# A routing table in SBUF, built from products of one-hot matrices, in a kernel of attention and two MoE layers

## The chip, the cores and the metric

The kernel runs on one core of a Trainium2 chip. The metric is the device time of one execution in microseconds. Engines: TensorE (PE in the profile; its weight loads are PEld), VectorE (DVE), ScalarE (ACT), GpSimd (POOL), and SyncE (SP), which issues most DMAs.

## The reference

Attention with a feature map, on 8 batches of 8 heads with 576 rows of 64, then two MoE layers on the 4608 rows of 512 that come out, each with 8 experts and one expert per row:

```python
def phi(x):
    proj = np.einsum('bhsd,df->bhsf', x, w_phi)
    proj = proj - np.max(np.abs(proj), axis=-1, keepdims=True)
    return np.concatenate([np.exp(proj), np.exp(-proj)], axis=-1)
q_p, k_p = (phi(q), phi(k))
kv = np.einsum('bhsf,bhsd->bhfd', k_p, v)
z = np.sum(k_p, axis=2)
num = np.einsum('bhsf,bhfd->bhsd', q_p, kv)
den = np.einsum('bhsf,bhf->bhs', q_p, z)[..., None] + 1e-06
...
logits = x @ w_gate + modality_bias[modality_id]
e_idx = np.argmax(logits, axis=1)
...
    h = np.maximum(x[mask] @ w1[e], 0.0)
    out[mask] = gate_w[mask, None] * (h @ w2[e])
```

The second layer is like the first, with another gate on its output. The inputs are float32.

## The kernel before

The work is written out in order by hand, so the order of the code is the order of each engine's queue. A small class `weave` holds chains of VectorE operations and puts a few of them between other work (`weave.step`), or all that is left of one (`weave.finish`).

**Attention** runs as 72 units, t = 9 b + s: in unit t the features of k for the s-th part of batch b are made (proj, km, kd, kp), while older units' sums over k (`kv_head`, line 1297, 128 columns per matmul) and output sums (`num`, line 1382, 65 columns) are under way. A unit of 8 heads x 4 chunks of v has its ones column apart, in `ONES`, so that the sum of k_p comes with the product. `num` ends in den, a reciprocal, and xt on VectorE (lines 1362 to 1366).

**Routing of a batch** is behind it: logits (`x_logits`, line 376), `finish` (softmax, one-hot matrix of the expert), `x_store` (rows to DRAM, line 1537), `x_ranks` (matmuls, lines 337 and 339), `places` (VectorE, lines 345 to 360: for each row its place in a table of 36864 numbers, ordered by expert), `x_enter`. `enter` (line 365) is, per chunk of 128 rows, an indirect DMA of GpSimd that scatters 128 numbers of 4 bytes into one of several tables in DRAM; the number names the row. The tables are zeroed first (line 444). Batches 0 to 5 do this inside the units of the following batches (the finish at t = 9 b + 24 or 25, the scatter at 9 b + 26), batches 6 and 7 in a tail behind the units, between the first MoE tiles.

**MoE** runs over 40 tiles of 128 rows per layer. A tile gathers its rows by an indirect DMA (line 752) whose indices come from the table. Three tiles of the fullest expert come early: `early_rows` reads their part of the tables (line 562), `early_idx` makes indices. At the end `route_a` reads five whole tables back (line 620), and `route_b` picks from them by 30 matmuls with one-hot columns (line 699). Lines 782 to 784 and 802 to 806 are the tiles' matmuls. The second layer has its own tables and the same steps.

Of the kernel before, what the change touches and what calls it, by code (L numbers as in the profile page):

```python
# [23 lines left out]
F = 128  # L24
# [20 lines left out]
PI = 1.0 / PS  # L45
V = D + 1

ONES = 32 * D + 8 * V

CM = 5  # L50

# [2 lines left out]
def attention_two_moe(  # L54
# [13 lines left out]
    x2_d = dpool.tile([NSLOT * 128 + 1, XW], F32, name="x2_d")  # L68
    rows_of = [C1 * 128, NSLOT * 128]

    tab_d = [[dpool.tile([NROW, 1], F32, name=f"tab{n}_{k}") for k in range(K)] for n, K in enumerate((5, G))]

    whole = ((0, 1),)

# [36 lines left out]
    row_no = []  # L111
    for n in range(2):
# [6 lines left out]
        row_no.append(t.rearrange("p c t -> p (c t)").bitcast(F32))  # L119

    nxt = [iota(f"nxt{n}", [[NT, NE]]) for n in range(2)]
    row0 = iota("row0", [[NT, NE]])
# [219 lines left out]
    def places(ps, oh16, C, n, valid=None):  # L342

        pl = sp.tile([128, CM, NE], F32, tag="pl", name="pl")[:, 0:C]
        nc.vector.tensor_tensor(
            pl, ps[:, 0:C], nxt[n].unsqueeze(1).to_broadcast([128, C, NE]), op=ALU.add)
        nc.vector.tensor_tensor(nxt[n], nxt[n], ps[:, C], op=ALU.add)
        yield
        nc.vector.tensor_tensor(pl, pl, oh16[:, 0:C], op=ALU.mult)
        yield  # L350
        po = sp.tile([128, CM], F32, tag="po", name="po")[:, 0:C]
        nc.vector.tensor_reduce(out=po, in_=pl, op=ALU.add, axis=AX.X)
        yield
# [8 lines left out]
        return pi  # L362

    def enter(n, pi, c, r):
        nc.gpsimd.indirect_dma_start(
# [35 lines left out]
    v1s = [flat(f"v1_{i}", 4 * (ONES + D)) for i in range(2)]  # L401
    w_m = [[flat(f"w{w}_{i}", 8192) for i in range(2)] for w in range(2)]


# [113 lines left out]
    etab = [const.tile([128, len(tab_d[n]), E], F32, name=f"etab{n}") for n in range(2)]  # L518
    ereg = {}

    def early(n):
# [45 lines left out]
    def early_idx(n):  # L567
        s = sp.tile([128, E, 2], F32, tag="es", name="es")
        nc.vector.tensor_reduce(
            out=s, in_=etab[n].rearrange("p k c -> p k c").bitcast(F16).rearrange("p k (c t) -> p c t k", t=2),  # L570
            op=ALU.add, axis=AX.X)
        yield
        nc.vector.scalar_tensor_tensor(
            out=s[:, :, 1], in0=s[:, :, 0], scalar=128.0, in1=s[:, :, 1], op0=ALU.mult, op1=ALU.add)
        yield
        nc.vector.tensor_scalar(eidx[n], s[:, :, 1], float(rows_of[n]), None, op0=ALU.add)
        yield
# [113 lines left out]
    def route_b(n):  # L691


        tab16, sel, ntile, ex = routed[n, "a"]
        rows = state["pg"][:, 3, 0 : 2 * M].rearrange("p (t m) -> p t m", t=2)
        for x in range(2):
            for i, t in enumerate(tab16):
                for k in range(3):
                    nc.tensor.matmul(  # L699
                        rows[:, x], t[:, k, :, x], sel[:, k], start=(i == 0 and k == 0),  # L700
                        stop=(i == len(tab16) - 1 and k == 2))
        rs = rt(n, "rs", [128, M])
        nc.vector.tensor_scalar(rs, rows[:, 0], 128.0, float(rows_of[n]), op0=ALU.mult, op1=ALU.add)
        idx = rt(n, "idx", [128, M], I32, True)
        nc.vector.tensor_tensor(idx, rs, rows[:, 1], op=ALU.add)
# [412 lines left out]
    with ExitStack() as actx:  # L1118
# [3 lines left out]
        sm = actx.enter_context(tc.tile_pool(name="sm", bufs=2))  # L1122
        def vw(t, u):

            a = t[:, D * u : D * u + D]
            return bass.AP(a.tensor, a.offset, [a.ap[0], (ONES - D * u, 2), (1, D)])

        def v_rem(t):


            return view(t, F32, 32 * D, 4, 2, V)

        weave = Weave()

# [30 lines left out]
        def load_v(b, half):  # L1165
            v1 = v1s[b % 2]
            if b < 2 and not half:
                nc.gpsimd.memset(v1[:, ONES:], 1.0)
                nc.gpsimd.memset(v_rem(v1), 0.0)
                for t in range(2):  # L1170
                    nc.gpsimd.memset(v_rem(v1)[64 * t : 64 * t + 64, :, t, D:V], 1.0)
            for c in (2 * half, 2 * half + 1):
                nc.sync.dma_start(
                    out=view(v1, F32, 0, H, 4, D)[:, :, c],
                    in_=v[b, :, 128 * c : 128 * c + 128].rearrange("h p d -> p h d"))
# [113 lines left out]
        def kv_head(b, h):  # L1289

            v1, kp = v1s[b % 2], kps.pop((b, h))
            if h % 2 == 0:
                kvp[b] = bank("kv", F32, 2, 2, 2 * D)
            ps = kvp[b]
            for half in range(2):
                for c in range(4):
                    nc.tensor.matmul(  # L1297
                        ps[:, half, h % 2], kp[:, c, half, :], vw(v1, 4 * h + c),
                        start=(h % 2 == 0 and half == 0 and c == 0), stop=False)
            if h % 2:  # L1300
# [223 lines left out]

        def x_places(b):
            n = 4 + b % 2
            rows[b, "pi"] = yield from places(rows[b, "rk"], rows[b, "oh"], n, 0)

        def x_enter(b):
            pi = rows.pop((b, "pi"))  # L1530
            for c in range(4 + b % 2):
                enter(0, pi, c, 9 * (b // 2) + 4 * (b % 2) + c)

        def x_store(b):
            for c, r in rows[b]:
# [24 lines left out]
        for t in range(9 * B + 6):  # L1560
# [41 lines left out]
            if b + 2 < B and s in (5, 6):  # L1602
                load_qk(q_of(b + 2), qT[b + 2], s - 5)
            split_step(split0, weave, t, "load")
            ready = batch_at(23)
            if ready != B - 3:
                ready = batch_at(24)
                ready = None if ready == B - 3 else ready
            if ready is not None:
                weave.finish(chains.pop(("finish", ready)))  # L1610
                x_store(ready)
# [54 lines left out]
            for x in firsts[t][1:] if 4 <= t < 9 else []:  # L1666
                proj(q_proj(*x))
                q_max(*x)
            each(5, num)
            if at(18, 0) and at(18)[0] < B - 1:  # L1670
                x_logits(*at(18))
            if at(17, 0) and at(17)[0] < B - 1:
                a_T(*at(17))
            if ready is not None:
                x_ranks(ready)
                chains["places", ready] = weave.add(x_places(ready))
# [15 lines left out]
            weave.step()  # L1692
            if ready is not None:
                weave.finish(chains.pop(("places", ready)))
            entered = ready if ready == B - 3 else batch_at(26)
            if entered is not None and (entered, "pi") in rows:
                x_enter(entered)

            if t == 9 * B - 3:
                chains["early"] = weave.add(early(0))  # L1700
            if t == 9 * B - 2:
                weave.finish(chains.pop("early"))
                early_rows(0)
            if t == 9 * B + 1:
                done(early_idx(0))
                for i in range(E):
                    gather(0, i)
            if t in (9 * B + 1, 9 * B + 5):
# [41 lines left out]
        x_enter(last)  # L1750


    late = ctx.enter_context(tc.tile_pool(name="late", bufs=1))
# [85 lines left out]
```

## Time and profile before

| | us |
|---|---|
| runs: median (lowest, highest) | 1561.77 (1560.21, 1566.68) |
| profiled execution | 1563.24 |
| its span, first to last instruction | 1561.5 |
| TensorE busy | 1467.9 (94%) |
| VectorE busy | 746.4 (48%) |
| ScalarE busy | 553.4 (35%) |
| GpSimd busy | 228.3 (15%) |
| mean granted clock of TensorE | 0.958 |

The attention runs to about 536 us, the tail with the first tiles to about 590, the MoE layers from there. A busy share is a mean over all of it: what a stage waits for is read from the waits and windows of that stage. The clock is given as a share of 2.4 GHz; a mean between 0.5 and 1 in a window is a mixture of stretches at 1.2 and at 2.4 GHz.

### The profile page before, as it was taken

What the parts mean: (1) busy time and instruction counts of PE and PEld (TensorE: products, weight loads), DVE (VectorE), ACT (ScalarE), POOL (GpSimd) and SP (SyncE); (2) the same over time, 40 slices, a digit from 0 to 9 for tenths busy, and PEclk for the clock granted to TensorE, in tenths of its full rate; (3) what the DMA queues carried; (4) which work ended last, traced back from release to release, by engine and by line L of the source; (5) the groups of instructions that cost most, each with busy time, mean ns of one, the idle gap of its engine ahead of it and who ended that gap; (6) DMA issues with size and microseconds to landing.
All of it is one profiled execution on the core that took longest, in us unless ns stands there. A gap on an engine that the chain in (4) does not pass through costs nothing. (4 is left out here: it accounts for less than half of the span.)

```text
span 1561.5 us, 38909 instructions
## 1 busy us (share of the span) xinstructions
PE 1467.9 (94%) x15626; PEld 1157.4 (74%) x15626; DVE 746.4 (48%) x2255; ACT 553.4 (35%) x850; POOL 228.3 (15%) x273
## 2 busy tenths in 40 slices
PE   6999998987999879999999999799889999999998
PEld 4999998987989847667777776466657777777775
DVE  3668776757756434646665666354341111111111
ACT  1346565554555403334444444243211111111111
POOL 1000101101011121202211211120131211211221
PEclk8999998989989889999999999899999999999999
DMA  8255656677431753657667777678945353484381
GB/s 250 92 159 164 142 170 157 174 168 136 124 62 49 265 84 114 158 185 201 204 213 178 195 180 230 113 199 244 306 150 174 76 150 104 133 272 138 81 281 43
DMA packets 158268, 254.40 MB, mean 163 GB/s; under 512 B 90953, under 2 KB 95613, under 8 KB 152192
## 3 DMA queue, kind: packets, MB, share of 16 engines
q1 hardware_dynamic: 141264, 210.22, 50.2%
q0 software_dynamic: 14784, 41.44, 7.9%
q8 instruction: 127, 2.08, 0.7%
q14 instruction: 61, 0.50, 0.1%
q10 hardware_dynamic: 2032, 0.16, 0.1%
HBM read 428.60 MB, written 83.22 MB: 328 GB/s over the span
## 5 line engine op out<-in xcount | busy, mean ns | idle before, releaser
L784 PE MATMUL proj<-xT,w 128*128 128x128 f16 x896 | 154.8, 221 | 10.4 <-issue 10.4
L783 PE MATMUL proj<-xT,w 128*128 128x128 f16 x896 | 154.7, 221 | 6.1 <-issue 6.1
L782 PE MATMUL proj<-xT,w 128*128 128x128 f16 x896 | 154.6, 220 | 3.2 <-issue 3.2
L802 PE MATMUL num<-w,qs 128*128 128x512 f32 x336 | 151.6, 605 | 0.0
L794 DVE SCALAR_TENSOR_TENSOR qs<-proj,qs 128x512 f16<-128x512 f32 x54 | 37.4, 692 | 228.3 <-ACT qs L793 228.3
L784 PEld LDWEIGHTS <-w 128*128 128x128 f16 x1344 | 132.2, 98 | 18.6 <-issue 18.6
L802 PE MATMUL num<-ks,qs 128*128 128x512 f32 x304 | 140.1, 614 | 4.2 <-DMA ks<-in_moe_w_dram 4.2
L1382 PE MATMUL num<-kvsb,E 128*128 128x65 f32 x1024 | 129.6, 282 | 11.9 <-DVE xt L1366 11.8
L782 PE MATMUL proj<-xT,v 128*128 128x128 f16 x816 | 138.7, 219 | 0.7 <-DVE xT L771 0.7
L784 PE MATMUL proj<-xT,v 128*128 128x128 f16 x816 | 138.7, 219 | 0.2 <-issue 0.2
L783 PE MATMUL proj<-xT,v 128*128 128x128 f16 x816 | 138.7, 219 | 0.0
L782 PEld LDWEIGHTS <-w 128*128 128x128 f16 x1344 | 132.1, 98 | 8.4 <-issue 4.4
L1382 PEld LDWEIGHTS num<-kvsb,E 128*128 128x128 f32 x1024 | 125.6, 200 | 14.9 <-issue 8.3
L1297 PE MATMUL kv<-v,kp 128*128 128x128 f32 x1024 | 135.7, 288 | 0.5 <-issue 0.5
L783 PEld LDWEIGHTS <-w 128*128 128x128 f16 x1344 | 132.1, 98 | 4.0 <-issue 2.0
L752 POOL DMA_INDIRECT xg<-x_d,idx x74 | 77.6, 1049 | 388.7 <-PE px L371 189.5
L1297 PEld LDWEIGHTS kv<-v,kp 128*128 128x128 f32 x1024 | 126.6, 201 | 1.6 <-issue 1.6
L783 PEld LDWEIGHTS <-v 128*128 128x128 f16 x1216 | 118.9, 98 | 3.1 <-issue 1.0
L782 PEld LDWEIGHTS <-v 128*128 128x128 f16 x1216 | 118.9, 98 | 2.5 <-issue 0.4
L784 PEld LDWEIGHTS <-v 128*128 128x128 f16 x1216 | 118.9, 98 | 0.0
L802 PEld LDWEIGHTS num<-w,qs 128*128 128x128 f32 x336 | 63.3, 193 | 72.0 <-issue 72.0
L1205 PE MATMUL proj<-wps,ks 64*128 64x128 f32 (+1 forms) x640 | 113.9, 301 | 0.9 <-issue 0.6
(328 smaller groups left out, 3366.7 us busy)
## 6 DMA issues: line engine op xcount, KB each, us to landing
w<-pl SPq DMA_DIRECT2D x114, 1024.0 KB
v<-pl SPq DMA_DIRECT2D x80, 1024.0 KB
ks<-in_moe_w_dram SPq DMA_DIRECT2D x40, 1024.0 KB
ks<-pl SPq DMA_DIRECT2D x40, 1024.0 KB
w<-in_moe_w_dram SPq DMA_DIRECT2D x38, 1024.0 KB
wf<-in_moe_w_dram SPq DMA_DIRECT2D x64, 512.0 KB
pl<-wo SPq DMA_DIRECT2D x52, 512.0 KB
w<-in_moe_w_dram SPq DMA_DIRECT2D x32, 512.0 KB
```

The source lines that it names most:

```text
L752: nc.gpsimd.indirect_dma_start(out=xg(n, i), out_offset=None, in_=src[n][0:nr, :], in_offset=bass.IndirectOffsetOnAxis(ap=ix, axis=0), bou ...
L782: nc.tensor.matmul(h[:, j], wk[:, 0, cs], xT[:, k], start=(k == 0), stop=False)
L783: nc.tensor.matmul(h[:, j], wk[:, 0, cs], xT[:, 4 + k], start=False, stop=False)
L784: nc.tensor.matmul(h[:, j], wk[:, 1, cs], xT[:, k], start=False, stop=(k == 3))
L794: nc.vector.scalar_tensor_tensor(out=lo, in0=h, scalar=0.0, in1=hi, op0=ALU.max, op1=ALU.subtract)
L802: nc.tensor.matmul(y, h[:, k], wk, start=(k == 0), stop=(k == 7))
L1205: nc.tensor.matmul(*a, **kw)
L1297: nc.tensor.matmul(ps[:, half, h % 2], kp[:, c, half, :], vw(v1, 4 * h + c), start=(h % 2 == 0 and half == 0 and c == 0), stop=False)
L1382: nc.tensor.matmul(ps[:, c, 0:V], e[:, half, 128 * c : 128 * c + 128], kw(g, half), start=(half == 0), stop=(half == 1))
```

## The change

1. The first layer's table lies in SBUF as `tab0`, [96, 3, 128] in f16. A number's place p is split into p & 127 and the rest (three more VectorE operations in `places`). For each chunk, `hots` makes two one-hot matrices: 128 x 128, scaled by a code of the row, and 128 x 288. `tab_add` multiplies them on TensorE, three matmuls per chunk, and `tab_out` adds the result to `tab0` on VectorE. Nothing of it goes through DRAM; the five tables of this layer, their zeroing, their scatters and their reads are gone. The second layer keeps its tables.
2. Picking: three matmuls (`tab_pick`), then three VectorE operations that turn the f32's bits into a row number (`decode`), for the early tiles and for `route_b`.
3. Places: batches 0 to 5 finish all at t = 9 b + 24 (s = 6); the one-hots are finished and multiplied at 9 b + 25 (s = 7), ahead of `num`. The early tiles' indices come one unit earlier.
4. In units with s = 1, `num` comes behind `x_logits` and `a_T`.
5. v lies with 65 columns per unit, its own ones column among them, so the matmuls of the sums over k have 65 columns in place of 128.
6. The tail: batch 6's logits of the last batch come first, then one-hots and table; behind batch 7's ranks, places, one-hots and table follow with no tile between.

```diff
+    tab0 = const.tile([96, 3, 128], F16, name="tab0")
+    nc.gpsimd.memset(tab0, 0.0)
...
+        nc.vector.tensor_scalar(pi, pi, 127, None, op0=ALU.bitwise_and)
+        pk = sp.tile([128, CM], F32, tag="pk", name="pk")[:, 0:C]
+        nc.vector.tensor_copy(pk, pi)
+        nc.vector.tensor_tensor(po, po, pk, op=ALU.subtract)
+        return pk, po
+    def hots(at_, pk, po, c0, mems):
+        out_ = []
+        at_.append(out_)
+        for c, m in enumerate(mems):
+            a, o = m[:, 0:128], m[:, 128:416]
+            nc.vector.tensor_scalar(
+                a, iota128, pk[:, c : c + 1], code[:, c0 + c : c0 + c + 1], op0=ALU.is_equal, op1=ALU.mult)
+            nc.vector.tensor_scalar(o, iota_c, po[:, c : c + 1], None, op0=ALU.is_equal)
+            out_.append((a, o))
+            yield
+    def tab_add(tag, hs_):
+        ps = bank(tag, F32, 3, 128)
+        for k in range(3):
+            for i, (a, o) in enumerate(hs_):
+                nc.tensor.matmul(
+                    ps[0:96, k], o[:, 96 * k : 96 * k + 96], a, start=(i == 0), stop=(i == len(hs_) - 1))
+        return ps
+    def tab_out(ps):
+        nc.vector.tensor_tensor(tab0, tab0, ps[0:96], op=ALU.add)
+    def decode(out_, ps, tag, w):
+        bits = sp.tile([128, w], I32, tag=tag, name="bits", bufs=1)
+        nc.vector.tensor_scalar(bits, ps.bitcast(I32), 13, None, op0=ALU.logical_shift_right)
+        nc.vector.tensor_scalar(bits, bits, -1.0, float((137 << 10) + 5119), op0=ALU.mult, op1=ALU.add)
+        nc.vector.tensor_scalar(out_, bits, float(rows_of[0]), None, op0=ALU.min)
...
+    def tab_pick(ps, sel):
+        for k in range(3):
+            nc.tensor.matmul(ps, tab0[:, k], sel[:, k], start=(k == 0), stop=(k == 2))
...
+        if n == 0:
+            tab_pick(rows[:, 0], sel)
+            done(decode(idx, rows[:, 0], "bits", M))
...
-            a = t[:, D * u : D * u + D]
-            return bass.AP(a.tensor, a.offset, [a.ap[0], (ONES - D * u, 2), (1, D)])
+            return t[:, V * u : V * u + V]
...
-                        ps[:, half, h % 2], kp[:, c, half, :], vw(v1, 4 * h + c),
+                        ps[:, half, h % 2, 0:V], kp[:, c, half, :], vw(v1, 4 * h + c),
...
-            for c in range(4 + b % 2):
-                enter(0, pi, c, 9 * (b // 2) + 4 * (b % 2) + c)
+        def x_enter(b, tag="qf"):
+            rows[b, "pt"] = tab_add(tag, rows.pop((b, "hots")))
...
-            ready = batch_at(23)
-            if ready != B - 3:
-                ready = batch_at(24)
-                ready = None if ready == B - 3 else ready
+            ready, entered = [(t - x) // 9 if (t - x) % 9 == 0 and 0 <= (t - x) // 9 < B - 2 else None for x in (24, 25)]
...
-            each(5, num)
+            if entered is not None:
+                weave.finish(chains.pop(("hots", entered)))
+                x_enter(entered)
+                tab_out(rows.pop((entered, "pt")))
+            if s != 1:
+                each(5, num)
             if at(18, 0) and at(18)[0] < B - 1:
                 x_logits(*at(18))
             if at(17, 0) and at(17)[0] < B - 1:
                 a_T(*at(17))
+            if s == 1:
+                each(5, num)
...
-            entered = ready if ready == B - 3 else batch_at(26)
-            if entered is not None and (entered, "pi") in rows:
-                x_enter(entered)
+                chains["hots", ready] = weave.add(x_hots(ready))
+                weave.step(2)
...
-        x_enter(last - 1)
-        tiles()
         for c in range(n):
             x_logits(last, c)
+        done(x_hots(last - 1))
+        x_enter(last - 1)
+        tab_out(rows.pop((last - 1, "pt")))
+        tiles()
...
         done(x_places(last))
-        x_enter(last)
+        done(x_hots(last))
+        x_enter(last, "num2")
+        tab_out(rows.pop((last, "pt")))
```

How the order moves. VectorE's queue of before, from batch 4's places (L352, po; L360, pi) into the next unit (den and xt finish an output sum, km and kd belong to k, nm to q):

```order
L352 TENSOR_REDUCE po<-pl 128x4
L244 SCALAR_TENSOR_TENSOR wo<-w_1_155,sb,wo 128x1024
L360 CAST pi<-po 128x4
L1362 TENSOR_SCALAR den<-num 128x4
L1268 TENSOR_REDUCE km<-proj 128x4
L1364 RECIPROCAL den<-den 128x4
L1225 TENSOR_REDUCE nm<-proj 128x4
L1366 TENSOR_TENSOR xt<-num,den 128x4x64
L1274 TENSOR_TENSOR kd<-proj,km 128x512
L1449 TENSOR_REDUCE xm_4850<-xmx 128x4
```

VectorE's queue of the changed kernel, from the same unit's xt and kd on (line numbers are those of the changed file: L1443 is xt, L1351 kd; L392 and L394 make the one-hots, in borrowed memory called kd):

```order
L1443 TENSOR_TENSOR xt<-num,den 128x4x64
L1351 TENSOR_TENSOR kd<-proj,km 128x512
L199 TENSOR_SCALAR pb<-pb 128x5
L1521 TENSOR_REDUCE xmx<-xt 128x4
L202 TENSOR_SCALAR sb<-pb 128x5
L203 TENSOR_SCALAR xi<-pb 128x5
L392 TENSOR_SCALAR kd<-iota_81,pk,code 128x128
L394 TENSOR_SCALAR kd<-iota_c,po 128x288
```

Three more pairs of L392 and L394 follow, and `tab_out`; before, these places held no such operation, and batch 4's entry was on GpSimd.

TensorE's queue of before, behind the ranks of batch 7 in the tail (L339 are the last ranks, L782 the first matmuls of a tile):

```order
L339 MATMUL pl<-oh_6363,ones_81 128x16
L339 LDWEIGHTS ones_81
L339 MATMUL pl<-oh_6363,ones_81 128x8
L782 LDWEIGHTS w_0_154
L782 MATMUL kv<-xT_145,w_0_154 128x128
```

TensorE's queue of the changed kernel at that place (L351 are the ranks, L402 the matmuls of `tab_add`, weights first):

```order
L351 MATMUL pl<-oh_6480,ones_76 128x16
L351 LDWEIGHTS ones_76
L351 MATMUL pl<-oh_6480,ones_76 128x8
L402 LDWEIGHTS kprem
L402 MATMUL num_6524<-kprem 96x128
```

Where a tile's matmuls stood behind the ranks, the table's matmuls stand now, 15 of them, and the tile comes behind those.

## Rows read from the trace of the kernel before

**Rows 1.** The page, part 1: engines, busy us, share of the span, instructions.

```profile
PE 1467.9 (94%) x15626; PEld 1157.4 (74%) x15626; DVE 746.4 (48%) x2255; ACT 553.4 (35%) x850; POOL 228.3 (15%) x273
```

**Rows 2.** TensorE's waits from 150 to 540 us: total us, times, longest.

```profile
PE num L1382 <- DVE xt L1366: 9.2, 10, 2.5
PE proj L1205 <- issue: 8.3, 4, 7.4
PE pl L376 <- issue: 4.3, 2, 3.7
PE qf L1340 <- issue: 3.6, 3, 1.5
PE qf L1205 <- issue: 3.0, 1, 3.0
PE px L371 <- issue: 1.7, 1, 1.7
```

**Rows 3.** TensorE's waits from 540 to 600 us.

```profile
PE proj L783 <- issue: 6.1, 3, 4.5
PE proj L782 <- issue: 2.0, 3, 1.1
...
PE proj L784 <- issue: 0.8, 2, 0.4
```

**Rows 4.** Timeline, 379 to 392 us: start, duration, engine, line, operation.

```profile
382.19 0.61 PE L371 MATMUL px<-ident,rows_f 128*128 128x128 f16 x8
...
390.56 0.37 PE L1205 MATMUL proj<-wps,qs 64*128 64x128 f32 x1 [7.36 <-issue]
```

**Rows 5.** Timeline of SyncE and of GpSimd, 361 to 377 us.

```profile
361.64 0.38 SPq L1537 DMA_DIRECT2D x_d<-rows_f  x1
...
370.02 1.02 POOL L365 DMA_INDIRECT tab<-row_no,pi  x1 [1.15 <-DVE den L1362]
...
375.16 1.50 POOL L365 DMA_INDIRECT tab<-row_no,pi  x1 [0.30 <-issue]
```

**Rows 6.** Windows of 20 us: busy time by engine; clock, DMA share, GB/s.

```profile
260.00:280.00 20.00, 19.54 (x205) 18.97 (x207) 11.57 (x28) 11.79 (x20) 1.24 (x1) 0.79 0.67 157
...
320.00:340.00 20.00, 18.84 (x185) 17.62 (x185) 12.22 (x28) 13.02 (x20) 0.00 (x0) 0.67 0.57 135
380.00:400.00 20.00, 11.80 (x131) 10.84 (x130) 8.50 (x21) 8.05 (x13) 0.00 (x0) 0.74 0.75 98
440.00:460.00 20.00, 17.09 (x162) 16.05 (x161) 8.70 (x23) 11.77 (x19) 0.00 (x0) 0.82 0.25 35
520.00:540.00 20.00, 20.00 (x252) 19.26 (x250) 11.69 (x43) 8.59 (x16) 0.22 (x3) 0.72 0.98 376
```

**Rows 7.** Timeline of TensorE: first and last of five num waits at s = 1.

```profile
142.75 1.41 PE L1382 MATMUL num<-kvsb,E 128*128 128x65 f32 x11 [1.31 <-DVE xt L1366]
...
454.87 1.30 PE L1382 MATMUL num<-kvsb,E 128*128 128x65 f32 x10 [1.20 <-DVE xt L1366]
```

**Rows 8.** The page, part 5: num and kv matmuls.

```profile
L1382 PE MATMUL num<-kvsb,E 128*128 128x65 f32 x1024 | 129.6, 282 | 11.9 <-DVE xt L1366 11.8
...
L1297 PE MATMUL kv<-v,kp 128*128 128x128 f32 x1024 | 135.7, 288 | 0.5 <-issue 0.5
```

**Rows 9.** Timeline of TensorE in the tail, 572 to 594 us.

```profile
572.81 7.09 PE L802 MATMUL num<-w,qs 128*128 128x512 f32 x16
...
580.36 0.23 PE L699 MATMUL qf<-ks,tab 96*128 96x40 f16 x3 [0.28 <-issue]
...
583.67 9.85 PE L802 MATMUL num<-w,qs 128*128 128x512 f32 x16
```

**Rows 10.** Timeline of VectorE: two operations at 13.3 and 556 us.

```profile
13.30 0.28 DVE L123 TENSOR_SCALAR tri<-iota,iota_p 128x128 f16<-128x128 f32 x1
...
556.06 0.46 DVE L627 TENSOR_TENSOR v<-v,iota_t 128x288 f32<-128x288 f32 x1
```

**Rows 11.** Timeline, 428 to 438 us, batch 4: VectorE and TensorE.

```profile
430.42 0.16 DVE L360 CAST pi<-po 128x4 int32<-128x4 f32 x1
...
433.69 1.90 PE L1382 MATMUL num<-kvsb,E 128*128 128x65 f32 x16
...
433.77 0.16 DVE L191 TENSOR_SCALAR xi<-pb 128x5 f32<-128x5 f32 x1
```

More of the change, by code (lines that the diff above doesn't have):

```diff
@@ L46 @@
 V = D + 1
-ONES = 32 * D + 8 * V
+VW = 40 * V
 CM = 5
@@ L69, in attention_two_moe @@
     rows_of = [C1 * 128, NSLOT * 128]
-    tab_d = [[dpool.tile([NROW, 1], F32, name=f"tab{n}_{k}") for k in range(K)] for n, K in enumerate((5, G))]
+    tab_d = [[dpool.tile([NROW, 1], F32, name=f"tab{n}_{k}") for k in range(K)] for n, K in enumerate((0, G))]
     whole = ((0, 1),)
@@ L109, in attention_two_moe @@
     nc.gpsimd.iota(col_no, [[96, 3]], base=1, channel_multiplier=1, allow_small_or_imprecise_dtypes=True)
-    row_no = []
-    for n in range(2):
+    row_no = [None]
+    for n in (1,):
         nc_ = rows_of[n] // 128
@@ L119, in attention_two_moe @@
         row_no.append(t.rearrange("p c t -> p (c t)").bitcast(F32))
+    tab0 = const.tile([96, 3, 128], F16, name="tab0")
+    nc.gpsimd.memset(tab0, 0.0)
+    code = const.tile([128, 5, 8], F32, name="code")
+    nc.gpsimd.iota(code, [[0, 5], [-128, 8]], base=2047, channel_multiplier=-1, allow_small_or_imprecise_dtypes=True)
+    for g in range(4):
+        nc.vector.tensor_scalar(code[:, g], code[:, g], float(1 << (4 - g)), None, op0=ALU.mult)
+    code = code.rearrange("p g c -> p (g c)")
+    iota_c = const.tile([128, NROW // 128], F16, name="iota_c")
+    nc.gpsimd.iota(iota_c, [[128, NROW // 128]], base=0, channel_multiplier=0, allow_small_or_imprecise_dtypes=True)
     nxt = [iota(f"nxt{n}", [[NT, NE]]) for n in range(2)]
@@ L361, in places @@
         yield
-        return pi
+        if n == 1:
+            return pi
+        nc.vector.tensor_scalar(pi, pi, 127, None, op0=ALU.bitwise_and)
+        yield
+        pk = sp.tile([128, CM], F32, tag="pk", name="pk")[:, 0:C]
+        nc.vector.tensor_copy(pk, pi)
+        yield
+        nc.vector.tensor_tensor(po, po, pk, op=ALU.subtract)
+        yield
+        return pk, po
[8 more added lines that the diff above has]
+            out_.append((a, o))
+            yield
+    def tab_add(tag, hs_):
[10 more added lines that the diff above has]
+        nc.vector.tensor_scalar(bits, ps.bitcast(I32), 13, None, op0=ALU.logical_shift_right)
+        yield
+        nc.vector.tensor_scalar(bits, bits, -1.0, float((137 << 10) + 5119), op0=ALU.mult, op1=ALU.add)
+        yield
+        nc.vector.tensor_scalar(out_, bits, float(rows_of[0]), None, op0=ALU.min)
+        yield
     def enter(n, pi, c, r):
@@ L400, in attention_two_moe @@
     ks_m = [flat(f"ks{i}", 2 * H * S) for i in range(2)]
-    v1s = [flat(f"v1_{i}", 4 * (ONES + D)) for i in range(2)]
+    v1s = [flat(f"v1_{i}", 4 * VW) for i in range(2)]
     w_m = [[flat(f"w{w}_{i}", 8192) for i in range(2)] for w in range(2)]
@@ L517, in attention_two_moe @@
     eidx = [const.tile([128, E], I32, name=f"eidx{n}") for n in range(2)]
-    etab = [const.tile([128, len(tab_d[n]), E], F32, name=f"etab{n}") for n in range(2)]
+    etab = [None, const.tile([128, len(tab_d[1]), E], F32, name="etab1")]
     ereg = {}
@@ L565, in early_rows, with early_sel, early_idx @@
                     "e (c p) -> p (e c)", p=128))
[L567 to L572, printed above, removed]
-        nc.vector.scalar_tensor_tensor(
[L574 to L577, printed above, removed]
+    def early_sel():
+        ec = sp.tile([128, E], F32, tag="ec", name="ec")
+        nc.vector.tensor_scalar(ec, iota_m[:, 0:E], 1.0, None, op0=ALU.add)
+        nc.vector.scalar_tensor_tensor(
+            out=ec, in0=eno[0][:, 0:1].to_broadcast([128, E]), scalar=float(C1), in1=ec, op0=ALU.mult, op1=ALU.add)
+        sel = sp.tile([96, 3, E], F16, tag="esel", name="esel")
+        nc.vector.tensor_tensor(
+            sel, ec[0:96].unsqueeze(1).to_broadcast([96, 3, E]), col_no.unsqueeze(2).to_broadcast([96, 3, E]),
+            op=ALU.is_equal)
+        return sel
+    def tab_pick(ps, sel):
+        for k in range(3):
+            nc.tensor.matmul(ps, tab0[:, k], sel[:, k], start=(k == 0), stop=(k == 2))
+    def early_idx(n, ps=None):
+        if n == 0:
+            yield from decode(eidx[0], ps, "ebits", E)
+        else:
+            s = sp.tile([128, E, 2], F32, tag="es", name="es")
+            nc.vector.tensor_reduce(
+                out=s, in_=etab[n].rearrange("p k c -> p k c").bitcast(F16).rearrange("p k (c t) -> p c t k", t=2),
+                op=ALU.add, axis=AX.X)
+            yield
+            nc.vector.scalar_tensor_tensor(
+                out=s[:, :, 1], in0=s[:, :, 0], scalar=128.0, in1=s[:, :, 1], op0=ALU.mult, op1=ALU.add)
+            yield
+            nc.vector.tensor_scalar(eidx[n], s[:, :, 1], float(rows_of[n]), None, op0=ALU.add)
+            yield
         nc.vector.tensor_tensor(wes[n], winv[:, n, 0], winv[:, n, 1], op=ALU.mult)
@@ L695, in route_b @@
         rows = state["pg"][:, 3, 0 : 2 * M].rearrange("p (t m) -> p t m", t=2)
[L696 to L703, printed above, removed]
-        idx = rt(n, "idx", [128, M], I32, True)
-        nc.vector.tensor_tensor(idx, rs, rows[:, 1], op=ALU.add)
+        idx = rt(n, "idx", [128, M], I32, True)
+        if n == 0:
+            tab_pick(rows[:, 0], sel)
+            done(decode(idx, rows[:, 0], "bits", M))
+        else:
+            for x in range(2):
+                for i, t in enumerate(tab16):
+                    for k in range(3):
+                        nc.tensor.matmul(
+                            rows[:, x], t[:, k, :, x], sel[:, k], start=(i == 0 and k == 0),
+                            stop=(i == len(tab16) - 1 and k == 2))
+            rs = rt(n, "rs", [128, M])
+            nc.vector.tensor_scalar(rs, rows[:, 0], 128.0, float(rows_of[n]), op0=ALU.mult, op1=ALU.add)
+            nc.vector.tensor_tensor(idx, rs, rows[:, 1], op=ALU.add)
         nti = rt(n, "nt", [1, 1], I32, True)
@@ L1123, in vw @@
         def vw(t, u):
[L1125 to L1126 removed]
+            return t[:, V * u : V * u + V]
         def v_rem(t):
[L1131 removed]
+            return view(t, F32, 32 * V, 4, 2, V)
         weave = Weave()
@@ L1167, in load_v @@
             if b < 2 and not half:
-                nc.gpsimd.memset(v1[:, ONES:], 1.0)
+                nc.gpsimd.memset(view(v1, F32, 0, 32, V)[:, :, D:V], 1.0)
                 nc.gpsimd.memset(v_rem(v1), 0.0)
@@ L1173, in load_v @@
                 nc.sync.dma_start(
-                    out=view(v1, F32, 0, H, 4, D)[:, :, c],
+                    out=view(v1, F32, 0, H, 4, V)[:, :, c, 0:D],
                     in_=v[b, :, 128 * c : 128 * c + 128].rearrange("h p d -> p h d"))
@@ L1526, in x_places, with x_hots @@
             n = 4 + b % 2
-            rows[b, "pi"] = yield from places(rows[b, "rk"], rows[b, "oh"], n, 0)
-        def x_enter(b):
-            pi = rows.pop((b, "pi"))
-            for c in range(4 + b % 2):
-                enter(0, pi, c, 9 * (b // 2) + 4 * (b % 2) + c)
+            rows[b, "pk"] = yield from places(rows[b, "rk"], rows[b, "oh"], n, 0)
+        def x_hots(b):
+            n = 4 + b % 2
+            if b < B - 2:
+                areas = [wk.tile([128, 4 * F], F32, tag="kd", name="kd"),
+                         wk.tile([128, 8, 128], F16, tag="xT", name="xT", bufs=1).rearrange("p a b -> p (a b)")]
+            else:
+                areas = [io.tile([128, 4, 2, F], F32, tag="kprem", name="kprem", bufs=1).rearrange("p a b c -> p (a b c)")]
+            mems = []
+            for a in areas:
+                a = a if a.dtype == F16 else a.bitcast(F16)
+                mems += [a[:, 416 * i : 416 * i + 416] for i in range(a.shape[1] // 416)]
+            mems = mems[0:4]
+            if n == 5:
+                mems.append(sm.tile([128, 416], F16, tag="hot", name="hot", bufs=1))
+            at_ = []
+            pk, po = rows.pop((b, "pk"))
+            yield from hots(at_, pk, po, 9 * (b // 2) + 4 * (b % 2), mems)
+            rows[b, "hots"] = at_[0]
+        def x_enter(b, tag="qf"):
+            rows[b, "pt"] = tab_add(tag, rows.pop((b, "hots")))
         def x_store(b):
@@ L1703, in attention_two_moe @@
                 early_rows(0)
-            if t == 9 * B + 1:
-                done(early_idx(0))
+            if t == 9 * B - 1:
+                esel = early_sel()
+            if t == 9 * B:
+                ps = p_small[:, 384 : 384 + E]
+                tab_pick(ps, esel)
+                done(early_idx(0, ps))
                 for i in range(E):
```

## The prediction

> **What bounds the kernel now.** I read the profile page first: TensorE is busy in 94% of the span, VectorE in 48%, GpSimd in 15% [rows 1]. So TensorE sets the time, and a change can win it time in three ways: take matmul time away, take its waits away, or take away the stretches at the lower clock. Then I read TensorE's waits. From 150 to 540 us, five groups are put down to "issue", which means that nothing in the trace releases them: 8.3 + 4.3 + 3.6 + 3.0 + 1.7 = 20.9 us. One group waits for VectorE: the num matmuls for xt, 9.2 us in 10 waits [rows 2]. From 540 to 600 us, "issue" costs 6.1 + 2.0 + 0.8 = 8.9 us [rows 3].
>
> What are the issue waits? The longest is 7.36 us, up to 390.56 [rows 4]. The last thing that GpSimd did before it is a row of five indirect DMAs of 4-byte numbers, 370.02 to 376.66 [rows 5], 6.5 us ahead of the start of the wait; the other long waits also follow such a group. I read them so: the scattered small writes hold up the DMA engines, and TensorE's own instructions come late. This is a correlation. The rows of the batch were stored earlier still, at 361.64 [rows 5], so the store remains a suspect.
>
> The granted clock is the other half. A clock of c over a 20 us window loses (1 - c) x 20 us of full-speed work: 4.2, 6.6, 5.2, 3.6 and 5.6 us in the five windows around and behind the waits [rows 6]. At 380 to 400 most of the low clock lies in the wait itself, so I count 2.0 there: together 22.0 us.
>
> **What the change removes.** All scatters of the first layer go. If they cause the issue waits, 20.9 us go, and the 22.0 us of low clock behind them: 42.9.
>
> At s == 1 the num matmuls now stand behind eight logits matmuls and eight transposes. Five waits are of this kind, the first at 142.75 (1.31 us) and the last at 454.87 (1.20 us) [rows 7]; the five sum to 4.9. The work that fills them takes over 1 us (the eight transposes alone 0.61 [rows 4]), so I take 4.5.
>
> The sums over k go from 128 columns to 65. The num matmuls already have 65 columns and the same 128-column weights: 1024 of them were busy 129.6 us, and the 1024 kv matmuls 135.7 [rows 8]. The whole difference is 6.1 us, which bounds the gain between 0 and 6.1; I take 4, since part of that difference is clock.
>
> The row that prices this edit lies far from a rule. The Trainium skill, page "TensorE: Matmul & The Clock Gate", section "Back-to-back issue gap", has the gap as the columns over the clock plus a few ns, so 63 columns fewer would save 26 ns in each of 1024 matmuls, 27 us in all (an estimate from that page). The rows contradict it here, since the 65-column group is nearly as slow; the same page of the Trainium skill, section "LDWEIGHTS (loading the stationary operand)" has a load of 128 columns take 107 ns, whatever the matmul has, and this fits them.
>
> In the tail the 8.9 us of issue waits go. The table's read goes with its matmuls: from the first of those to the next other one, 580.36 to 583.67, 3.3 us. The 16 num matmuls behind took 9.85 us, and the same 16 took 7.09 us ten us earlier [rows 9]: 2.8 us of clock. Together 15.0.
>
> **What it adds.** Per chunk, two VectorE operations make one-hot matrices. The nearest rows: 128x128 in 0.28 us, 128x288 in 0.46 us [rows 10]; the second now reads half-width numbers with a single operand, so between 0.28 and 0.46. Four chunks cost 2.2 to 3.0 us, and three small operations 0.16 each [rows 11]. TensorE adds 12 or 15 matmuls of 128 columns per batch; at 0.61 us for eight of that shape [rows 4] they are at most 0.9 to 1.1 us, at their spacing of 56 ns some 0.7 and 0.8.
>
> These are cheap, but TensorE must now wait for them, ahead of num, and before it waited for none of them. In batch 4 the places end at 430.58, VectorE's list for the unit ends at 433.93 (xi), and num begins at 433.69 [rows 11]. With the three small operations and the eight new ones ahead, VectorE ends at 433.9 + 0.5 + 2.2 to 3.0, 436.6 to 437.4, so TensorE waits 2.9 to 3.7 us; operations in a row overlap by some 0.08 us, which takes up to 1 us off. I take 2.6 from 1.9 to 3.7, and with the matmuls 3.3 us for each of batches 0, 2 and 4. Queued behind the waiting matmul on TensorE are num, then the projections of the next unit; VectorE's den, ScalarE's exponentials and the next km wait for those in turn. Odd batches 1 and 3 have a fifth chunk (0.6 more) and their finish is now flushed a unit earlier, about a dozen small operations at 0.16 to 0.19, 2.2 us more ahead of TensorE: 2.6 + 0.6 + 2.2 + 0.8 = 6.2. Batch 5 was early before too: 4.0. Sum: 9.9 + 12.4 + 4.0 = 26.3.
>
> After waits of 0.9 to 4 us the clock fell in some places and not in others; a window with a fall loses 3.6 to 6.6 us [rows 6]. From 0 to 6.6 us per batch I take 2.7, for waits of about 3 us: 16 in all. GpSimd's start work gets longer by a few operations; they lie beside TensorE's first loads, and half a us is its cost if that cover is gone.
>
> In the tail two waits are new. Batch 6: eight one-hot operations with only five chunks' logits to cover them, 2.4 + 0.7. Batch 7: no tile stands between its ranks and its matmuls, so places (five operations), three more and ten one-hots lie bare: 18 operations at 0.16 to 0.46, 3.3 to 5.0; I take 3.3, because such operations overlap, + 0.8. Together 7.2, so the tail gains 15.0 - 7.2 = 7.8.
>
> **The sum.** 42.9 + 4.5 + 4 + 7.8 = 59.2 gained; 26.3 + 16 = 42.3 lost; net -17. The profiled execution took 1563.2 us, 1.5 above the median of the runs; 1563.2 - 17 = **1546 us**. The MoE layers keep the scatters of the second layer and their waits; instruction addresses shift, so those may move by a few us either way.
>
> **Rivals.**
> *The new waits eat the gain* (0.18). With the long ends of the waits (3.7 in place of 2.6, six times, +6.6) and a fall of the clock behind half of them more (+7), 1560. For it: VectorE is nearly full in just those units. Against: these are ends, all at once.
> *TensorE stands before the one-hots and each stand drops the clock* (slower, 0.15). At 6.6 us of clock for each of six batches in place of 2.7 the loss grows by 23.4, and the net is +6; with waits at their long end +13: 1570 to 1576. It decides as soon as a batch loses more than 59.2 / 6 = 9.9 us. For it: windows with a clock of 0.67 and 0.79 behind 3 to 4 us of waits [rows 6]. Against: short waits of 0.9 us often cost nothing more.
> *The scatters aren't the cause* (0.06): the row stores or instruction supply by themselves make the waits. Then 42.9 and 8.9 are not gained: 1546 + 52 = 1598. For it: the stores come a unit before every scatter, and remain. Against: they land without waits in the 7 us before the scatters.
> A rule that bears on this: the Trainium skill, page "DMA: Bandwidth & Descriptors", section "Specifications", has transfers under 512 bytes done as read-modify-write; if so, 4-byte writes are the dear ones. No row here separates the two.
> *The waits are covered* (0.10): VectorE reaches the one-hots early, as its list has slack in some batches. Then 26.3 shrinks to the matmuls' 4.3 and the clock costs nothing: 1546 - 22 - 16 = 1508 at most; half of it is 1527.
> *The columns count in full* (0.03): if the 1024 matmuls fell to the spacing of their columns, half their 135.7 us, and half of that were on the path, 34 - 4 less: 1516. The Trainium skill's page on the clock gate, named above, would have it so.
>
> **How the numbers follow.** The forecast's own case has 0.48, with a range of 1533 to 1555 (gains 5 us either way, clock 0 to 5 more). Chances: forecast 0.48, the two fast ones 0.13, within 1.5% the "eaten" case 0.18, slower 0.15 + 0.06. A measurement tells a change from none at about 0.5%, 7.8 us. Some of the eaten case lies below 1554, so faster 0.63, same 0.17, slower 0.20. The range for 8 in 10 takes in the eaten case, half the covered case and the lower part of the slower one: 1526 to 1571.
>
> **What would show it.** Right: no issue waits of over 1 us between 150 and 540, a clock of 0.9 or more at 260 to 280, 320 to 340 and 520 to 540, and in their place, near 180, 240, 300, 370, 430 and 490 us, a wait of TensorE for the one-hots (the matmuls that write qf), 2 to 4 us each; the num matmuls at s == 1 with no wait; kv's busy time near num's. Wrong: issue waits that stay without scatters, waits for the one-hots of over 4 us, or a clock of 0.7 behind them.

## The result, and the profile after

The changed kernel took 1577.38 us (median of 10 runs, 1565.68 to 1582.18) against 1559.13 us for the kernel before (10 runs, 1548.51 to 1567.72). The ratio is 1.0104, with a 95% interval of 1.0065 to 1.0144: about 1% slower, where 1.1% faster was forecast. The profiled execution took 1576.54 us. Of a kernel's runs, those more than 1.5% above its fastest count as slow; the ratios below leave them out while the medians keep them, which matters for before_v65 (three of six runs, the profiled one among them) and scatters_back (two of twelve, likewise).

The page of the changed kernel, parts 1 and 2 (busy us and share; the granted clock in 40 slices):

```profile
PE 1510.4 (96%) x15710; PEld 1201.6 (76%) x15710; DVE 770.5 (49%) x2365; ACT 553.0 (35%) x850; POOL 194.2 (12%) x239
...
PEclk7699897988979689999999999999999999999999
```

TensorE is busier than in [rows 1], by 42.5 us, and yet the time is longer. So look at the clock, in the second row: low at the start, and low in a slice again and again up to the fifteenth. TensorE's waits of the changed kernel, 150 to 540 us (total, times, longest):

```profile
PE num L1459 <- DVE xt L1443: 10.6, 11, 2.6
PE qf L402 <- DVE kd L394: 5.3, 5, 2.6
PE qf L402 <- DVE xT L394: 0.8, 4, 0.2
PE qf L402 <- DVE hot L394: 0.4, 2, 0.2
```

The first thing to see is what isn't there: none of the issue waits, which were 20.9 us in [rows 2]. The waits for the one-hots (the matmuls into qf) sum to 6.5 us, far less than the forecast's terms. From 540 to 620 us the issue waits of [rows 3] are gone too, and the table's matmuls wait:

```profile
PE num L402 <- DVE kprem L394: 2.7, 4, 2.1
PE pl L431 <- DVE nxt L359: 1.0, 1, 1.0
```

Then the windows of 100 us of the changed kernel (busy time of PE, PEld, DVE, ACT, POOL; clock; DMA share; GB/s):

```profile
0.00:100.00 100.00, 86.57 (x619) 77.22 (x619) 42.69 (x111) 20.95 (x39) 7.15 (x41) 0.76 0.49 146
100.00:200.00 100.00, 96.17 (x1075) 91.89 (x1077) 78.13 (x205) 54.02 (x93) 0.70 (x2) 0.94 0.52 165
200.00:300.00 100.00, 95.48 (x1075) 91.00 (x1071) 71.21 (x187) 55.35 (x92) 1.60 (x2) 0.90 0.50 148
300.00:400.00 100.00, 92.98 (x961) 88.02 (x959) 72.97 (x210) 47.19 (x80) 1.08 (x2) 0.85 0.47 150
400.00:500.00 100.00, 98.11 (x1077) 93.39 (x1074) 69.96 (x186) 57.43 (x96) 0.35 (x1) 0.91 0.26 85
500.00:600.00 100.00, 91.95 (x869) 84.03 (x869) 55.08 (x229) 32.34 (x56) 4.18 (x7) 0.76 0.41 150
```

TensorE's busy times sum to 561.3 us; the same windows of the kernel before sum to 540.4, so the changed kernel idles 20.8 us less. The clocks tell the rest. Each (1 - c) x 100 is work lost: 24 + 6 + 10 + 15 + 9 + 24 = 88 us. For the kernel before the clocks in these windows are 0.90, 0.98, 0.95, 0.88, 0.93 and 0.85, a loss of 51. The 37 us more of lost clock outweigh the waits that went. Some of either loss lies in waits, where a low clock costs nothing, so these sums are rough.

Where does the time go? In both kernels the last output sums of the attention end where a tile's transposes (px) begin, and from there on TensorE has the same number of matmuls but for one, so the two profiles can be cut at that place. First the place, in the kernel before and in the changed one:

```profile
530.49 0.93 PE L371 MATMUL px<-ident,xg 128*128 128x128 f16 x8
```

```profile
562.01 0.62 PE L426 MATMUL px<-ident,xg 128*128 128x128 f16 x8
```

and the windows up to it and behind it, again before and after:

```profile
0.00:530.50 530.50, 483.40 (x5168) 454.43 (x5168) 347.73 (x940) 257.20 (x438) 40.52 (x79) 0.92 0.56 149
530.50:1561.50 1031.00, 984.48 (x10460) 702.93 (x10459) 398.64 (x1315) 296.20 (x412) 187.78 (x194) 0.98 0.60 170
```

```profile
0.00:562.00 562.00, 528.66 (x5251) 498.40 (x5251) 365.98 (x1023) 256.68 (x438) 14.94 (x54) 0.85 0.45 143
562.00:1574.80 1012.80, 981.78 (x10461) 703.17 (x10459) 404.56 (x1343) 296.32 (x412) 179.23 (x185) 0.98 0.58 170
```

Up to this place the changed kernel is 31.5 us slower, though TensorE idles 13.8 us less: its clock is 0.85 against 0.92. Behind it, in the tail and the MoE layers, it is 18.2 us faster, 15.5 of that idle time.

One unit in full, batch 4, the stretch of [rows 11]. TensorE's timeline of the changed kernel (start, duration, operation):

```profile
442.83 1.95 PE L1374 MATMUL kv<-v,kp 128*128 128x65 f32 x16
445.75 1.97 PE L1459 MATMUL num<-kvsb,E 128*128 128x65 f32 x16 [0.96 <-DVE xt L1443]
...
449.94 3.62 PE L1374 MATMUL kv<-v,kp 128*128 128x65 f32 x16
...
454.33 0.59 PE L402 MATMUL qf<-kd 128*96 128x128 f16 x2
...
456.48 3.62 PE L1459 MATMUL num<-kvsb,E 128*128 128x65 f32 x16
```

and a window on it:

```profile
448.00:465.00 17.00, 16.76 (x108) 15.57 (x107) 11.38 (x38) 4.25 (x9) 0.00 (x0) 0.50 0.17 65
```

The clock fell some 2 us after a wait of 0.96 us ahead of num, which the kernel before has too. There, at a clock of 0.90 over 17 us, it is 3.4 us at 1.2 GHz:

```profile
426.48 1.97 PE L1382 MATMUL num<-kvsb,E 128*128 128x65 f32 x16 [0.92 <-DVE xt L1366]
```

```profile
428.00:445.00 17.00, 17.00 (x179) 16.29 (x178) 12.63 (x36) 10.21 (x17) 3.94 (x4) 0.90 0.61 106
```

In the changed kernel TensorE was busy for 16.76 of 17.00 us, waited for nothing of note, and stayed at 1.2 GHz all the while: a group of 16 kv matmuls took 3.62 us in place of 1.95. The table's matmuls, at 454.33, hardly wait here, since TensorE itself is late. This is why the waits for one-hots are so short in the view of waits: the low clock hides them.

### The profile page after: what moved, and what is told of

It reads as the page before. It is cut to its first block, busy times and chain, and to the rows that moved or that the text cites. A ratio compares the mean times of both kernels' runs of the same rounds, so it can differ in the third digit from the quotient of the medians.

```text
span 1574.8 us, 39025 instructions
## 1 busy us (share of the span) xinstructions
PE 1510.4 (96%) x15710; PEld 1201.6 (76%) x15710; DVE 770.5 (49%) x2365; ACT 553.0 (35%) x850; POOL 194.2 (12%) x239
## 5 line engine op out<-in xcount | busy, mean ns | idle before, releaser
L1459 PE MATMUL num<-kvsb,E 128*128 128x65 f32 x1024 | 144.1, 301 | 12.8 <-DVE xt L1443 12.7
L1459 PEld LDWEIGHTS num<-kvsb,E 128*128 128x128 f32 x1024 | 139.0, 218 | 15.4 <-issue 11.2
L1374 PE MATMUL kv<-v,kp 128*128 128x65 f32 x1024 | 140.4, 296 | 0.0
L1374 PEld LDWEIGHTS kv<-v,kp 128*128 128x128 f32 x1024 | 134.8, 212 | 0.6 <-issue 0.6
L1282 PE MATMUL proj<-wps,ks 64*128 64x128 f32 (+1 forms) x640 | 120.3, 314 | 0.3 <-DVE nm L1302 0.3
```

Of the source, the lines that this page charges most:

```text
L1282: nc.tensor.matmul(*a, **kw)
L1374: nc.tensor.matmul(ps[:, half, h % 2, 0:V], kp[:, c, half, :], vw(v1, 4 * h + c), start=(h % 2 == 0 and half == 0 and c == 0), stop=False)
L1459: nc.tensor.matmul(ps[:, c, 0:V], e[:, half, 128 * c : 128 * c + 128], kw(g, half), start=(half == 0), stop=(half == 1))
```

## The experiments

Ratios are to the kernel before, run beside each on the same chip. Clocks are those of the windows 0 to 600 us of the profiled execution, and the last column sums (1 - c) x 100 over the six.

| kernel | median us | ratio (95%) | clock by 100 us | lost us |
|---|---|---|---|---|
| before | 1550.84 and 1553.52 | 1 | 0.90 0.98 0.95 0.88 0.93 0.85 | 51 |
| the change | 1577.38 | 1.0104 (1.0065 to 1.0144) | 0.76 0.94 0.90 0.85 0.91 0.76 | 88 |
| kv128 | 1536.17 | 0.9894 (0.9864 to 0.9924) | 0.90 0.97 0.95 0.91 0.97 0.97 | 33 |
| before_v65 | 1596.59 | 1.0205 (1.0152 to 1.0258) | 0.88 0.95 0.85 0.85 0.81 0.76 | 90 |
| hots_late | 1539.27 | 0.9926 (0.9892 to 0.9961) | 0.83 0.98 0.91 0.88 0.93 0.91 | 56 |
| kv128_hots_late | 1516.25 | 0.9763 (0.9734 to 0.9792) | 0.98 0.98 0.98 0.99 0.97 0.95 | 15 |
| scatters_back | 1548.55 | 0.9951 (0.9922 to 0.998) | 0.91 1.00 0.93 0.93 0.91 0.87 | 45 |
| num128 | 1512.39 | 0.9747 (0.9711 to 0.9783) | 0.95 1.00 0.98 1.00 1.00 0.98 | 9 |
| kv96 | 1535.21 | 0.9897 (0.9859 to 0.9935) | 0.91 0.97 0.97 0.91 0.97 0.86 | 41 |
| num_first | 1525.9 | 0.9836 (0.9798 to 0.9874) | 0.95 0.98 0.91 0.95 0.97 0.93 | 31 |

The profiled executions of before_v65 (1609.46 us) and scatters_back (1556.38) lie above their medians, so their clocks are on the low side. The median of the change is from another chip than the others (1559.13 before it), so it is compared by ratios; the others are from two chips, as the two medians of the kernel before show, and are compared by ratios too.

These clocks are of one profiled execution each, but the mean clock of every run is on record too. It is 0.936 to 0.948 in the ten runs of the changed kernel, 0.923 to 0.945 in the six of before_v65, 0.956 to 0.967 in the runs of the kernel before beside the experiments, 0.968 to 0.974 in kv128 and 0.976 to 0.983 in kv128_hots_late. A run's time multiplied by its mean clock is 1468 to 1505 us in all of them, while the times go from 1508 to 1620: most of the differences in time are differences in clock.

The first question was which of two parts brings the clock down: the narrow matmuls (N) or the new waits for the one-hots (W).

**kv128.** The matmuls of the sums over k stream 128 columns again, and nothing else is changed:

```diff
-            return t[:, V * u : V * u + V]
+            return t[:, V * u : V * u + 2 * D]
...
-                        ps[:, half, h % 2, 0:V], kp[:, c, half, :], vw(v1, 4 * h + c),
+                        ps[:, half, h % 2], kp[:, c, half, :], vw(v1, 4 * h + c),
```

> The changed kernel, but each matmul of the sums over k streams 128 columns again: its own 65 and 63 of its neighbours', whose products nobody reads. Theory N (the narrow matmuls keep the clock down after any short wait): the stretches at 1.2 GHz get short again, the loss to them in attention falls from 63 us to 25 to 35, and the time is about 1540 to 1550 us, faster than before the change. Rival W (the new waits for the one-hots bring the clock down, the columns don't matter): the waits are all there, so the time stays at 1572 to 1580.

1536 us: the columns cost 1.0104 - 0.9894 = 2.1%, some 33 us. Now the waits show. Its timeline at the unit of above, and two windows on it:

```profile
428.76 1.97 PE L1459 MATMUL num<-kvsb,E 128*128 128x65 f32 x16 [0.91 <-DVE xt L1443]
...
432.10 2.00 PE L1374 MATMUL kv<-v,kp 128*128 128x128 f32 x16
...
437.12 0.26 PE L402 MATMUL qf<-kd 128*96 128x128 f16 x1 [2.57 <-DVE kd L394]
...
439.08 3.62 PE L1459 MATMUL num<-kvsb,E 128*128 128x65 f32 x16
```

```profile
428.00:437.00 9.00, 5.79 (x61) 5.48 (x61) 7.79 (x33) 4.11 (x7) 0.00 (x0) 1.00 0.49 189
439.00:446.00 7.00, 7.00 (x52) 6.88 (x50) 2.57 (x4) 0.00 (x0) 0.00 (x0) 0.51 0.20 77
```

The same short wait for xt (0.91 us) stands first, and the clock doesn't fall there. It falls behind the wait of 2.57 us for the one-hots, to 0.51 from 439 to 446, and is back after 7 us, where it took 17 above. The layout of v is still that of the change, so it is the columns, not the layout, that cost the time. TensorE's waits of kv128, 150 to 600 us:

```profile
PE qf L402 <- DVE kd L394: 12.3, 10, 2.6
PE num L1459 <- DVE xt L1443: 10.5, 11, 2.5
```

The waits for one-hots, 12.3 us in the largest group, were 5.3 in the changed kernel, and the kernel is faster all the same.

**before_v65.** The other way round: the kernel before with v's layout and the 65 columns alone (the v parts of the diff of the change, nothing else).

> The kernel before with part of the change alone: v laid out with 65 columns per unit and the sums over k in 65 columns. N: the stretches at 1.2 GHz get longer, the first one from about 22 to 69 us as in the changed kernel, and the time rises by 15 to 30 us, to 1574 to 1590. W: no new wait is there, so the time stays or falls by up to 4 us.

2.05% slower by the ratio, 32 us, a little more than expected, though the edit adds no wait. The start isn't as expected: in its profile the first stretch at 1.2 GHz ends at 46 us, not at 69 (before: 22 to 33 and 36 to 43). It lost its clock later, 90 us against 51. The rows of its num and kv matmuls:

```profile
L1381 PE MATMUL num<-kvsb,E 128*128 128x65 f32 x1024 | 147.5, 306 | 21.2 <-DVE xt L1365 19.8
...
L1296 PE MATMUL kv<-v,kp 128*128 128x65 f32 x1024 | 141.3, 297 | 0.0
```

The kv matmuls were busy 141.3 us where 128 columns took 135.7 [rows 8]. This execution also waited longer for xt (19.8 us, where [rows 8] has 11.8), so its profile isn't the columns alone; but all six runs have a lower mean clock than any of the kernel before.

**hots_late.** The changed kernel with the table's matmuls behind num:

```diff
-            if entered is not None:
-                weave.finish(chains.pop(("hots", entered)))
-                x_enter(entered)
-                tab_out(rows.pop((entered, "pt")))
             if s != 1:
                 each(5, num)
+            if entered is not None:
+                weave.finish(chains.pop(("hots", entered)))
+                x_enter(entered)
+                tab_out(rows.pop((entered, "pt")))
```

> The changed kernel, but the table's matmuls stand behind num in the unit, so TensorE doesn't wait for the one-hots ahead of num. N: the waits of 10 us go at most, the long stretches at 1.2 GHz stay, since a wait of num for xt of 0.9 us comes ahead of each: 1566 to 1575 us. W: the falls of the clock go with the waits, about 1545 us.

1539 us: 1.8% or 28 us off the changed kernel, the rival's figure, so N alone fell too. Yet the narrow matmuls still show: its clock at the unit of batch 4 stays low in a busy stretch,

```profile
435.00:448.00 13.00, 13.00 (x85) 12.63 (x83) 9.10 (x31) 3.41 (x7) 0.00 (x0) 0.50 0.10 41
```

**kv128_hots_late.** Both edits.

> Both edits: 128 columns in the sums over k, and the table's matmuls behind num. N: like 128 columns alone, less some 5 us of waits, 1535 to 1545 us. W: like the later matmuls alone, about 1545, no better for the columns.

1516 us, 2.4% below the kernel before, and lower than either edit alone, below the expectation of both. So both theories hold, each for about half: from the changed kernel the two edits take 33 and 28 us, together 53 (1.0104 - 0.9763 = 3.4%). An overlap would be no wonder, since a wait that is gone can't bring the clock down, whatever the columns; but the 8 us between 61 and 53 are within the intervals of the ratios. Its waits, 150 to 600 us:

```profile
PE num L1459 <- DVE xt L1443: 16.4, 17, 2.5
PE num L402 <- DVE kprem L394: 2.7, 4, 2.1
```

Waits of num for xt (16.4 us) are what is left; the loss of clock is down to 15 us.

**scatters_back.** That kernel with the scatters of the first layer beside its table:

```diff
+            for c in range(4 + b % 2):
+                r = 9 * (b // 2) + 4 * (b % 2) + c
+                nc.gpsimd.indirect_dma_start(
+                    out=tab_x[c][:, :], out_offset=bass.IndirectOffsetOnAxis(ap=pi[:, c : c + 1], axis=0),
+                    in_=row_no[1][:, r : r + 1], in_offset=None, bounds_check=NROW - 1, oob_is_err=False)
```

> The kernel with 128 columns in the sums over k and the table's matmuls behind num, and beside its table in SBUF the first layer's scatters again: per chunk an indirect DMA of 128 numbers of 4 bytes into tables in DRAM, which nobody reads. Theory S (the scatters make TensorE's issue waits): issue waits of 15 to 30 us come back between 150 and 600 us, and the time is 1530 to 1555 us against 1516 without them. Rival (the stores of the rows, which every kernel here has, or chance make the waits): no more issue waits than without, 1513 to 1520 us.

29 us slower by the ratios (0.9951 against 0.9763). The scatters are dear, and the stores of rows, which both kernels have, don't make this difference. The way is only partly the expected one. From 150 to 600 us these are the largest issue waits, and above them a wait for a tile's gather that the kernel without the scatters doesn't have:

```profile
PE pl L428 <- DMA xg<-x_d,idx: 4.5, 1, 4.5
...
PE num L1284 <- issue: 2.8, 2, 2.2
...
PE num L1419 <- issue: 1.3, 1, 1.3
...
PE pl L433 <- issue: 1.0, 1, 1.0
```

All issue waits sum to 6.9 us, less than the 15 that were expected, and far less than the 20.9 and 8.9 of the kernel before [rows 2] [rows 3]. The lost clock rose from 15 to 45 us, 7 of that in the first 100 us, ahead of any scatter. Still, the profiles with scatters of the first layer (before, before_v65, this one) all have issue waits in this stretch, and the seven without them have none. In the kernel before the three longest (3.0, 3.7 and 7.4 us) begin 6 to 12 us behind the last scatter of a group; the zeroing of this layer's tables is over by then, and the reads of them have not begun. Why the same scatters make shorter issue waits here stays open.

**num128.** kv128_hots_late with 128 columns in num as well (the columns once from 0 and once from 1 on, so the denominators come last):

```diff
                         nc.tensor.matmul(
-                            ps[:, c, 0:V], e[:, half, 128 * c : 128 * c + 128], kw(g, half),
+                            ps[:, c], e[:, half, 128 * c : 128 * c + 128],
+                            bass.AP(a.tensor, a.offset, [a.ap[0], (1, 2), (1, D)]),
```

> The same kernel without the scatters, but num's matmuls have 128 columns too: the 64 columns, and columns 1 to 64 once more, of which only the last is read. If narrow matmuls keep the clock down wherever they stand, the loss to 1.2 GHz in attention falls from 14 us to 5 to 10, and the time is 1506 to 1513 us. If it is only kv's place, or if the wider matmuls cost what the clock gives back (0.05 to 0.12 us per group of 16, 3 to 8 us in all), 1516 to 1524.

0.9747 against 0.9763: within the intervals. The clock is the best of all (9 us lost), and the time gained isn't clear of noise.

**kv96.** The changed kernel with 96 columns (`V * u + 96` and `0:96` in the two lines of kv128).

> The changed kernel with 96 columns per matmul in the sums over k, its own 65 and 31 of its neighbours', whose products nobody reads. Theory N (columns against the clock): between the changed kernel (1567 us on this scale, ratio 1.010) and the one with 128 (1536, 0.989): ratio 0.993 to 1.006, with a loss to 1.2 GHz in attention between 31 and 63 us. Rival (the layout or one particular width matters): at either end.

0.9897, at the end of the wide ones: 96 columns do what 128 do, here, with the changed kernel's layout of v. So the loss doesn't grow evenly with what is cut. These are three widths in one kernel, and no rule is drawn from them.

**num_first.** kv128_hots_late with num ahead of logits and transposes at s = 1 again.

> The kernel with 128 columns and the table's matmuls behind num, and num ahead of the logits and transposes again in the units with s = 1. If that part of the change was worth its 4.5 us: 1518 to 1524 us, with waits of num for xt of 0.6 to 1.3 us at s = 1 where 0.57 stood. If it gives nothing: 1514 to 1518.

0.9836 against 0.9763: this part of the change is worth 0.7%, 11 us, more than the 4.5 expected. Its waits and those with num behind, at the first such unit of each:

```profile
139.08 1.19 PE L1459 MATMUL num<-kvsb,E 128*128 128x65 f32 x9 [1.30 <-DVE xt L1443]
```

```profile
136.01 2.00 PE L1459 MATMUL num<-kvsb,E 128*128 128x65 f32 x16 [0.57 <-DVE xt L1443]
```

The six waits at s = 1 sum to 7.4 us, against 2.9 with num behind: 4.5 us, the forecast's figure for this. The rest of the 11 goes with the clock, by one profile of each: 31 us lost against 15.

## Why the prediction was wrong

**Where it failed: the price of the columns.** The prediction bounded this edit between 0 and a gain of 6.1 us, by the busy times of kv and num [rows 8], and took a gain of 4. At full clock that holds: a group of 16 takes 1.95 us with 65 columns and 2.00 with 128, 3 us over 64 groups. The Trainium skill, page "TensorE: Matmul & The Clock Gate", section "Back-to-back issue gap", gives the formula by which 27 us would go (an estimate from that page) for an isolated gap alone, and says there that in a stream of weight loads and matmuls both set the spacing; the 1.95 and 2.00 us agree with that. But nothing in the sum allowed for a loss, and the loss is 32 or 33 us, by kv128 and before_v65 alike. The busy times of the changed kernel's groups show it:

```profile
L1459 PE MATMUL num<-kvsb,E 128*128 128x65 f32 x1024 | 144.1, 301 | 12.8 <-DVE xt L1443 12.7
...
L1374 PE MATMUL kv<-v,kp 128*128 128x65 f32 x1024 | 140.4, 296 | 0.0
```

The kv matmuls are narrower and num's are as they were, and both are busy for longer than in [rows 8]: a group of 16 takes 3.62 us in place of 1.95 in a stretch at 1.2 GHz, and more of them lie in such stretches. In the prediction's terms, the attention was to gain 51.4 (42.9 + 4.5 + 4) and lose 42.3, net a gain of 9; it lost 31.5 us by the profiles. The columns, forecast at +4 and measured at -33, are 37 of these 41 us.

**The second: the clock behind the new waits.** At full clock (kv128) four waits of 2.54 to 2.58 us stand where 2.6 was taken; batches 1 and 3 wait 2.53 and 1.46 us ahead of num at s = 6, where 2.2 was taken, and batch 5 waits 1.03. That is 15.3 us, and 4.3 of matmuls, where the term was 26.3: it was too large for batches 1, 3 and 5. For the clock behind them 16 us were taken. Putting the table's matmuls behind num gained 28 us with 65 columns and 20 with 128 (0.9894 - 0.9763), so the two terms of 42 together were too large; but with narrow matmuls the waits shrank (6.5 us, where kv128 has 14.9 ahead of the matmuls into qf) and the clock's share grew. The prediction's own sign of being wrong, a clock of 0.7 behind the waits, is there: 0.50 from 520 to 540 us, behind batch 5's wait for the one-hots.

**What held.** The scatters: forecast 42.9 us with the clock, and 8.9 in the tail; measured 29. That they are dear is shown; the size was too large: put back, they made 6.9 us of issue waits from 150 to 600 us, not 29.8, and why stays open. s = 1: 4.5 forecast, 4.5 of waits and 11 in all measured, with the clock. The one-hot operations cost what the bounds said:

```profile
L392 DVE TENSOR_SCALAR kd<-iota,pk,code 128x128 f16<-128x128 f32 x12 | 4.1, 338 | 0.0
...
L394 DVE TENSOR_SCALAR kd<-iota_c,po 128x288 f16<-128x288 f16 x12 | 3.4, 286 | 0.0
```

0.34 + 0.29 = 0.62 us per chunk, forecast 0.56 to 0.74. Behind the attention the forecast was a gain of 7.8, all of it in the tail, and nothing for the MoE layers; the profiles show 18.2, and it was not tried which part of the change gives the other 10. In the tail the issue waits went, and the 16 num matmuls behind are at full clock again, 7.09 us against the 9.85 of [rows 9]; the waits for one-hots there are shorter than the forecast's 5.7 us:

```profile
576.89 0.26 PE L402 MATMUL qf<-kprem 128*96 128x128 f16 x1 [0.45 <-DVE kprem L394]
...
592.17 0.26 PE L402 MATMUL num<-kprem 128*96 128x128 f16 x1 [2.11 <-DVE kprem L394]
...
602.09 7.09 PE L880 MATMUL num<-w,qs 128*128 128x512 f32 x16
```

**The rivals.** The slower one had a chance of 0.15 with the mechanism "each stand drops the clock"; that is about half of the loss. No rival had the narrow matmuls as a cost; the one that named the columns had them as a gain. In sum: gains of 59 were forecast, and scatters and s = 1 came to about 40; losses of 42 were forecast, and columns and one-hots came to 53. The net of some 13 us of loss stands against 16 measured (1.04% of 1559); the difference is within the intervals. The size of the miss is partly luck: the overpriced scatters and one-hots nearly cancelled, which left the columns bare.

What stays open: why narrow matmuls keep the clock down, and by which width; whether the start's long stretch at 1.2 GHz (21 to 69 us in the changed kernel, 22 to 33 and 36 to 43 before) is all theirs, since it varies between kernels that are alike there; and whether a scatter's cost lies in the write itself or in how the queue handles it.

## What to carry to other kernels

Before narrowing a matmul, ask what it does to the clock, not just to its own time: a narrowing that gains 3 us at 2.4 GHz lost 33 here, in stretches at 1.2 GHz in which TensorE was busy. A new wait on TensorE costs its length and, in some places here and not in others, a fall of the clock behind it, so put work that must wait for VectorE behind other matmuls that are ready. When a change has several parts, run each alone: here two parts gained some 40 us and two lost 53, and the best kernel keeps the first, and undoes the others by two small edits (2.4% faster than before).

## What the runs showed of the hardware

TensorE stayed at 1.2 GHz for 17 us in which it was busy 99% of the time, with 65-column f32 matmuls; with 128 columns in the sums over k, at the same unit and behind a longer wait, it was back after 7 us. Streaming 63 columns that nobody reads made this kernel 2% faster. Scatters of 4-byte numbers, 36 of them, cost a kernel 29 us; in one profile of each, the visible waits (6.9 us of issue, 4.5 for a gather) grew less than the lost clock (15 to 45 us).
